# The loads of a phase re-ordered, and two deferred mean projections pinned behind the first output matmuls

## The chip, the cores and the metric

The kernel runs on one core of one Trainium2 chip, as one program in one launch. The metric is the device time of the execution in microseconds (us). A kernel is timed in several executions, and the kernel before is always timed on the same chip in the same rounds.

## The reference

The kernel computes two independent parts from two inputs and puts their results side by side, `[1, 2048, 2048]` in bf16.

```python
# part A: a diagonal state-space layer (S5), x is [1, 2048, 1024]
h = Lam_bar * h + Bu[t]                              # for each of the 2048 steps t
y = 2.0 * einsum('blp,dp->bld', hseq, Cmat).real + x * Dskip

# part B: attention in 64 segments of 32 tokens, 32 heads of 128, with 8 memory tokens in front
h = concatenate([mem, xs])                           # 40 rows
q, k, v = h @ Wq, h @ Wk, h @ Wv
o = softmax(mask(q @ k.T * scale)) @ v @ Wo
mem = o[:8]                                          # memory of the next segment
# ... result: concatenate([y, o[8:] of all segments], axis=-1)
```

Part B's recurrence over the memory is avoided in this kernel: it guesses the memory of every segment from the mean of the segment's values, and checks the guess at the end. Those means are what this text calls a *mean group*: for 4 heads, 32 matmuls of 128x64 that multiply `Wv` by the mean token of each segment. The result (`b_ogT`) is multiplied by `Wo` in eight *Wo groups* to give the guess.

## The kernel before

Time runs through four phases. Phase 1 computes the states of part A (kept in device memory, `a_hs`) and most values of part B. **Phase 2**, about 361 to 495 us, is the one that the change touches: the output matmuls of part A, with the guess of part B woven in. Then come projections with attention, and the output projection.

Part A in phase 2 is a generator. It yields after each *half*: 16 matmuls of 128x512 into one PSUM buffer of the tag "O", and the eviction from PSUM into the output tile `a_ot`. Two halves make an output tile of 128 rows, which is then stored.

```python
    def ps(self, tag, shape=(128, 512), dt=FP32):
        return self.psp.tile(list(shape), dt, name="ps" + tag, bufs={"P": 3, "S": 2, "R": 1, "O": 2}[tag])
# ... (cut)
    def stage2(self, pool):
        k = self.k; V, G, PE = k.V, k.G, k.PE
        q0 = k.G
        # ... (cut: Dskip, and load_xn, which loads 128 rows of x into a_xn2, 3 buffers)
        for tb in range(NB):                        # 4 blocks of 512 rows
            hl = []
            for q in range(4):                      # states of the block: 4 tiles of 0.5 MB, 2 buffers
                hl.append(pool.tile([128, 2, 2, TB], BF16, name=f"a_hl{q}", bufs=2))
                (q0 if tb == 0 else k.SP).dma_start(hl[q][:], self.hs[tb][:, 2 * q:2 * q + 2, :, :])
            for tt in range(4):                     # 4 output tiles of 128 rows
                t0 = tb * TB + tt * 128
                xn = xns.pop(4 * tb + tt)
                xd = pool.tile([128, D], FP32, name="a_xd", bufs=2)
                G.tensor_tensor(xd[:], xn[:], dB[:], ALU.mult)
                ot = pool.tile([128, D], BF16, name="a_ot", bufs=2)
                for half in range(2):
                    hs = slice(half * 512, (half + 1) * 512)
                    py = k.ps("O")
                    # ... (cut: 16 matmuls of the states with CT into py)
                    V.tensor_tensor(ot[:, hs], py[:], xd[:, hs], ALU.add)
                    yield
                k.SP.dma_start(self.out[0, t0:t0 + 128, 0:D], ot[:])
                if 4 * tb + tt + 3 < TT:
                    load_xn(4 * tb + tt + 3, k.SP)
```

Note for later: `a_ot` has two buffers, the store of a finished tile is issued from SyncE (`k.SP`), and nearly all loads of the phase are issued from SyncE as well.

The body of the phase weaves the two deferred mean groups (`og`), the Wo groups (`guess`, which loads its four 2 MB pieces `b_wog` itself) and the first `Wq`/`Wk` load in between:

```python
            g = b.guess(p2)
            s2 = a.stage2(p2)
            wv = [wv, b.load_wv(1)]
            for i, _ in enumerate(s2):
                if i in (2, 4):
                    b.og(i // 2 - 1, wv[i // 2 - 1], "P")
                if i > 4 and i % 2 == 1:
                    next(g, None)
                if i == 16:
                    b.load_wqk(0)
            for _ in g:
                pass
            b.v_mem(0, wv[0])
            b.v_mem(1, wv[1])
```

The order of the source is not the order on the engines: a scheduler orders each engine's instructions, unless one is pinned with `keep_in_program_order`. In the kernel before it puts both deferred mean groups ahead of all halves.

Of the kernel before, what the change touches and what calls it, by code (L numbers as in the profile page):

```python
# [9 lines left out]
BF16 = mybir.dt.bfloat16  # L10
# [15 lines left out]
H = 32; E = 128; SEG = 32; M = 8; NSEG = 64; L = M + SEG  # L26
# [95 lines left out]
class PartA:  # L122
# [137 lines left out]
# [4 lines that stand above are left out]
        dB = pool.tile([128, D], BF16, name="a_dB", bufs=1)  # L264
        q0.dma_start(dB[:], self.Dskip.unsqueeze(0).to_broadcast([128, D]))
        xns = {}

        def load_xn(t, q):
            xns[t] = pool.tile([128, D], BF16, name="a_xn2", bufs=3)
            q.dma_start(xns[t][:], self.x[0][t * 128:(t + 1) * 128, :])  # L270
        for t in range(3):
            load_xn(t, q0)
        for tb in range(NB):
            hl = []
            for q in range(4):
                hl.append(pool.tile([128, 2, 2, TB], BF16, name=f"a_hl{q}", bufs=2))
                (q0 if tb == 0 else k.SP).dma_start(hl[q][:], self.hs[tb][:, 2 * q:2 * q + 2, :, :])
            for tt in range(4):
                t0 = tb * TB + tt * 128
                xn = xns.pop(4 * tb + tt)  # L280
# [6 lines that stand above are left out]
                    for pc in range(PC):  # L287
                        for i in range(2):
                            PE.matmul(py[:], hl[pc // 2][:, pc % 2, i, tt * 128:(tt + 1) * 128], self.CT[:, i, pc, hs],  # L289
                                      start=(pc == 0 and i == 0), stop=(pc == PC - 1 and i == 1))  # L290
                    V.tensor_tensor(ot[:, hs], py[:], xd[:, hs], ALU.add)  # L291
                    yield
                k.SP.dma_start(self.out[0, t0:t0 + 128, 0:D], ot[:])
                if 4 * tb + tt + 3 < TT:
                    load_xn(4 * tb + tt + 3, k.SP)



class PartB:
# [96 lines left out]
    def og(self, hb, w, tag="R"):  # L396
        k = self.k
        p = k.ps(tag)
        for h in range(4):
            for c in range(KC):  # L400
                k.PE.matmul(p[:, h * NSEG:(h + 1) * NSEG], w[:, c, h * 128:(h + 1) * 128], self.xbar[:, c, :], start=(c == 0), stop=(c == KC - 1))
        k.V.tensor_copy(self.ogT[:, hb * 4:(hb + 1) * 4, :], p[:, 0:4 * NSEG].rearrange("p (h s) -> p h s", h=4))


    def guess(self, pool):
        k = self.k; V, PE = k.V, k.PE
        pg = k.ps("S")
        for q in range(4):
            wo = pool.tile([128, H, 256], BF16, name="b_wog", bufs=2)
            k.SP.dma_start(wo[:], self.Wo[:, :, q * 256:(q + 1) * 256])  # L410
            for dc in range(2):
                c = 2 * q + dc
                for h in range(H):
                    PE.matmul(pg[:, c * NSEG:(c + 1) * NSEG], wo[:, h, dc * 128:(dc + 1) * 128], self.ogT[:, h, :], start=(h == 0), stop=(h == H - 1))
                yield
        pv = pg[:].rearrange("p (c s) -> p c s", c=KC)
        m = self.memT
        V.tensor_copy(m[:, :, NMX + 1:NMX + 2], pv[:, :, 0:1])
        V.tensor_copy(m[:, :, NMX + 3:NM], pv[:, :, 1:NSEG])

        gx = pool.tile([128, KC, NM], BF16, name="b_gx", bufs=1)
        V.tensor_copy(gx[:, :, 0:2], pv[:, :, 0:2])
        V.tensor_copy(gx[:, :, 2:NTL - 1], pv[:, :, 1:NSEG])
        V.tensor_copy(gx[:, :, NTL - 1:NM], pv[:, :, 0:1].to_broadcast([128, KC, NMX + 1]))
        pt = k.ps("R", (128, 1024), BF16)
        for c in range(KC):
            PE.transpose(pt[0:NM, c * 128:(c + 1) * 128], gx[:, c, :], k.ident[:])
        V.tensor_copy(self.gm[:], pt[0:NM, :])
        yield
# [325 lines left out]
def kernel_main(tc, A_x, A_Lre, A_Lim, A_Bre, A_Bim, A_Cre, A_Cim, A_logdt, A_Dskip, B_x, B_mem0, B_Wq, B_Wk, B_Wv, B_Wo, out,  # L755
                force=False, dbg=None):
    with ExitStack() as ctx:
        k = K(tc, ctx)
# [4 lines left out]
        b = PartB(k, B_x, B_mem0, B_Wq, B_Wk, B_Wv, B_Wo, out)  # L763

        def pool(name, side, bufs=2):
            return tc.tile_pool(name=name, bufs=bufs, side=side, reuse_waits="tile")
# [8 lines left out]
        with pool("p1", "right") as p1:  # L775
            a.tab = a.tmp = a.wp = a.btp = p1
            wv = b.load_wv(0)
# [9 lines left out]
            for pc in range(PC):  # L787
                v = b.v_x(pc, wv)
                nxt = None
                for tb in range(NB):  # L790
# [7 lines left out]
                    if tb == 1:  # L798
                        nxt = b.load_wv((pc + 1) % PC)
# [23 lines left out]
                wv = nxt  # L823
# [7 lines left out]
        with pool("p2", "right") as p2:  # L831
            g = b.guess(p2)
            s2 = a.stage2(p2)
            wv = [wv, b.load_wv(1)]
            for i, _ in enumerate(s2):
                if i in (2, 4):
                    b.og(i // 2 - 1, wv[i // 2 - 1], "P")
                if i > 4 and i % 2 == 1:
                    next(g, None)
                if i == 16:  # L840
                    b.load_wqk(0)
            for _ in g:
                pass
            b.v_mem(0, wv[0])
            b.v_mem(1, wv[1])
# [49 lines left out]
@with_exitstack  # L895
def kernel(
    ctx: ExitStack,
    tc: tile.TileContext,
    A_x: bass.AP,
    A_Lambda_re: bass.AP,  # L900
    A_Lambda_im: bass.AP,
    A_B_re: bass.AP,
    A_B_im: bass.AP,
    A_C_re: bass.AP,
    A_C_im: bass.AP,
    A_log_dt: bass.AP,
    A_Dskip: bass.AP,
    B_x: bass.AP,
    B_mem0: bass.AP,
    B_Wq: bass.AP,  # L910
    B_Wk: bass.AP,
    B_Wv: bass.AP,
    B_Wo: bass.AP,
    B_seg_len: bass.AP,
    out: bass.AP,
):
    assert int(B_seg_len) == SEG
    kernel_main(tc, A_x, A_Lambda_re, A_Lambda_im, A_B_re, A_B_im, A_C_re, A_C_im, A_log_dt, A_Dskip,
                B_x, B_mem0, B_Wq, B_Wk, B_Wv, B_Wo, out)
# [35 lines left out]
```

## Time and profile before

| kernel before | |
|---|---|
| time | 1315.48 us median of 3 runs (1314.9 to 1315.63) |
| profiled span, mean granted clock | 1312.2 us, 0.992 |
| TensorE busy, whole | 1267.0 us (97%) |
| phase 2, start of its first mean group to start of the memory values | 360.26 to 494.59, 134.33 us |
| TensorE idle in phase 2 | 11.4 us (134.33 less 122.95 busy) |

The busy table of the page (time, share of the span, instructions) says that TensorE is the engine to look at:

```profile
PE 1267.0 (97%) x7808; PEld 658.2 (50%) x7874; DVE 673.7 (51%) x1500; ACT 427.1 (33%) x1135; POOL 211.4 (16%) x291
```

The list of waits of TensorE in phase 2 (what waited, for what, total us, times, longest) has one large entry:

```profile
PE psP L401 <- DMA b_wv<-in_B_Wv_dram: 10.0, 1, 10.0
PE psP L401 <- ACT b_vst L62: 0.5, 1, 0.5
```

The timeline of TensorE shows where it lies (start, us, line, operation; in brackets the idle time before it and what ended it):

```profile
360.26 1.10 PE L401 MATMUL psR<-b_xbar,b_wv 128*128 128x64 bf16 x32
361.90 1.09 PE L401 MATMUL psP<-b_xbar,b_wv 128*128 128x64 bf16 x32 [0.54 <-ACT b_vst L62]
372.99 1.89 PE L401 MATMUL psP<-b_xbar,b_wv 128*128 128x64 bf16 x32 [9.99 <-DMA b_wv<-in_B_Wv_dram]
374.69 0.61 PE L289 MATMUL psO<-t_105,a_hl_3617 128*128 128x512 bf16 x1
...
494.59 3.62 PE L437 MATMUL psP<-b_wv,b_xe 128*73 128x512 bf16 x16
```

The third mean group stands 10 us for its `Wv`, and the output matmuls (`psO`), which need nothing of it, queue up behind it. The last line, the memory values (128x73), ends the phase.

The timeline of SyncE's queue shows the issues (start, how long the issue took, line, transfer). The `Wv` load goes out only at 367.07.

```profile
367.07 0.54 SPq L370 DMA_DIRECT2D b_wv<-in_B_Wv_dram  x1
367.93 0.38 SPq L410 DMA_DIRECT2D b_wog<-in_B_Wo_dram  x1
368.36 8.01 SPq L277 DMA_DIRECT2D a_hl_3928<-a_hs_71  x1
...
378.32 0.42 SPq L277 DMA_DIRECT2D a_hl_3934<-a_hs_71  x1
384.00 0.34 SPq L293 DMA_DIRECT2D out_dram<-a_ot  x1
```

Two evictions of VectorE in the phase:

```profile
383.28 0.69 DVE L291 TENSOR_TENSOR a_ot<-psO,a_xd 128x512 bf16<-128x512 f32 x1 [0.96 <-PE psO L289]
...
393.69 0.69 DVE L291 TENSOR_TENSOR a_ot<-psO,a_xd 128x512 bf16<-128x512 f32 x1 [2.82 <-PE psO L289]
```

The table of stretches of 6 us (length; busy us and instructions of PE, PEld, DVE, ACT, POOL; granted TensorE clock; share of the DMA engines; GB/s) shows the second cost of the gap, a clock of about half speed:

```profile
366.00:372.00 6.00, 0.00 (x0) 0.00 (x0) 0.10 (x1) 0.00 (x0) 0.00 (x0) 0.62 0.79 239
372.00:378.00 6.00, 4.79 (x40) 2.97 (x42) 0.42 (x1) 0.00 (x0) 0.00 (x0) 0.53 1.16 294
...
384.00:390.00 6.00, 5.95 (x29) 2.69 (x29) 0.69 (x1) 0.00 (x0) 2.13 (x1) 1.00 0.87 284
```

The Trainium skill ("TensorE: Matmul & The Clock Gate", Part 1) says that about 3.4 us of idling halves the clock and about 3.4 us of work restores it. The trace agrees in kind: TensorE idles from 363.0, the granted clock is 0.50 from about 368, and it is back at about 377.7, some 4.7 us after work resumed.

### The profile page before, as it was taken

The page shows a single profiled execution, that of the slowest core. Times are in us where ns is not written, and L with a number is a line of the kernel's source. Part 1 is how long each engine was busy: PE and PEld are TensorE (multiplying, and loading weights), DVE is VectorE, ACT ScalarE, POOL GpSimd, SP SyncE. Part 2 cuts the span into 40 slices and gives each one's busy share as a digit, 9 for nine tenths or more (in the row PEclk, how much of TensorE's full clock was granted, in tenths as well). Part 3 has the DMA queues.
Part 4 walks back from the last instruction along what each step waited for, and adds up shares of the span by engine and source line. Part 5 has one row for each costly group of instructions (what it writes and reads, how often), then busy time and mean ns, then how long its engine had stood idle before and what let it go on. Part 6 is the DMA issues. An engine that isn't in the chain of part 4 may idle for free. (4 is left out here: it accounts for less than half of the span.)

```text
span 1312.2 us, 20083 instructions
## 1 busy us (share of the span) xinstructions
PE 1267.0 (97%) x7808; PEld 658.2 (50%) x7874; DVE 673.7 (51%) x1500; ACT 427.1 (33%) x1135; POOL 211.4 (16%) x291
## 2 busy tenths in 40 slices
PE   6899899999969999999999999999999989999997
PEld 2344444444435545555555555555555544444443
DVE  6999998988821224555555555545555530001000
ACT  3333333343210001554544454544544540001000
POOL 5000000000112221222222222222222220000000
PEclk9999999999989999999999999999999989999999
DMA  9993443344389519323343434333333470403000
GB/s 227 262 215 105 121 127 101 110 129 144 121 263 311 172 48 262 85 84 110 99 133 99 133 99 133 99 87 98 86 90 78 142 240 18 136 18 127 16 21 21
DMA packets 230939, 163.15 MB, mean 124 GB/s; under 512 B 74976, under 2 KB 214864, under 8 KB 230840
## 3 DMA queue, kind: packets, MB, share of 16 engines
q1 hardware_dynamic: 229368, 158.18, 42.2%
q0 software_dynamic: 1408, 3.61, 0.9%
q8 instruction: 63, 1.03, 0.3%
q14 instruction: 36, 0.29, 0.1%
q10 hardware_dynamic: 64, 0.02, 0.0%
HBM read 95.72 MB, written 49.30 MB: 111 GB/s over the span
## 5 line engine op out<-in xcount | busy, mean ns | idle before, releaser
L383 PE MATMUL psP<-b_wv,b_xe 128*128 128x512 bf16 x1024 | 229.8, 381 | 16.0 <-DMA b_xe<-in_B_x_dram 11.2
L519 ACT ACTIVATE b_e<-psS 99x396 bf16<-99x396 f32 x176 | 88.2, 501 | 416.8 <-PE psS L516 413.6
L522 POOL TENSOR_TENSOR b_m<-b_e,maskB 99x396 bf16<-99x396 bf16 x160 | 139.4, 871 | 352.9 <-ACT b_e L519 352.9
L542 DVE TENSOR_TENSOR b_ot<-psO,b_r 128x384 bf16<-128x384 f32 x176 | 98.1, 558 | 189.2 <-ACT b_r L536 170.4
L383 PEld LDWEIGHTS <-b_xe 128*128 128x128 bf16 x1024 | 100.0, 98 | 139.3 <-DMA b_xe<-in_B_x_dram 12.7
L607 PEld LDWEIGHTS <-b_ol 128*128 128x128 bf16 x896 | 87.8, 98 | 106.3 <-issue 1.7
L64 DVE CAST b_ost<-psP 128x512 bf16<-128x512 f32 x16 | 11.1, 692 | 193.4 <-PE psP L607 193.4
L62 ACT ACTIVATE b_vst<-psP 128x512 bf16<-128x512 f32 x128 | 73.8, 586 | 97.0 <-PE psP L383 82.8
L607 PE MATMUL psP<-t_4704,b_ol 128*128 128x512 bf16 x438 | 99.6, 381 | 0.7 <-issue 0.2
L607 PE MATMUL psP<-wo_12095,b_ol 128*128 128x512 bf16 x438 | 98.8, 379 | 0.5
L536 ACT ACTIVATE b_r<-b_ln 128x396 f32<-128x396 f32 x176 | 94.0, 534 | 5.4
L535 ACT ACTIVATE b_ln<-psR 128x396 f32<-128x396 f32 x176 | 86.9, 494 | 0.0
L62 ACT ACTIVATE b_ost<-psP 128x512 bf16<-128x512 f32 x16 | 9.6, 597 | 211.2 <-PE psP L607 198.0
L291 DVE TENSOR_TENSOR a_ot<-psO,a_xd 128x512 bf16<-128x512 f32 x32 | 22.1, 692 | 95.6 <-PE psO L289 88.2
L64 DVE CAST b_k_4709<-psP 128x480 bf16<-128x480 f32 (+2 forms) x96 | 48.8, 529 | 31.1 <-PE psP L492 30.6
L540 PE MATMUL psO<-b_m,b_v 99*128 99x99 bf16 x704 | 61.4, 209 | 0.8 <-DMA b_v<-b_vx_74 0.8
L531 PE MATMUL psR<-b_m,ones 99*128 99x396 bf16 x176 | 59.2, 336 | 3.1 <-POOL b_m L522 2.2
L64 DVE CAST b_k_4717<-psP 128x480 bf16<-128x480 f32 (+2 forms) x96 | 48.7, 528 | 21.2 <-PE psP L492 21.2
L540 PEld LDWEIGHTS <-b_v 99*128 99x128 bf16 x704 | 50.6, 98 | 14.3 <-DMA b_v<-b_vx_74 1.1
L64 DVE CAST b_q_4705<-psP 128x480 bf16<-128x480 f32 (+2 forms) x96 | 48.7, 528 | 17.2 <-PE psP L492 17.2
L64 DVE CAST b_q_4713<-psP 128x480 bf16<-128x480 f32 (+2 forms) x96 | 48.6, 528 | 12.5 <-PE psP L492 12.5
L248 ACT ACTIVATE a_gr<-a_wr 128x512 bf16<-128x512 f32 x32 | 20.2, 630 | 72.1 <-DVE a_wr L237 72.1
(724 smaller groups left out, 1950.2 us busy)
## 6 DMA issues: line engine op xcount, KB each, us to landing
b_wv<-in_B_Wv_dram SPq DMA_DIRECT2D x16, 1024.0 KB
b_wog<-in_B_Wo_dram SPq DMA_DIRECT2D x4, 2048.0 KB
out_dram<-a_ot SPq DMA_DIRECT2D x16, 256.0 KB
t_4704<-in_B_Wo_dram SPq DMA_DIRECT2D x1, 4096.0 KB
b_ol<-b_os_90 SPq DMA_DIRECT2D x4, 1024.0 KB
b_ol<-b_os_91 SPq DMA_DIRECT2D x4, 1024.0 KB
b_ol<-b_os_92 SPq DMA_DIRECT2D x4, 1024.0 KB
wo_12095<-in_B_Wo_dram SPq DMA_DIRECT2D x1, 4096.0 KB
```

The lines of the kernel that those rows point to most:

```text
L62: self.S.activation(out, in_, ACT.Copy)
L64: self.V.tensor_copy(out, in_)
L291: V.tensor_tensor(ot[:, hs], py[:], xd[:, hs], ALU.add)
L383: k.PE.matmul(p[:], self.xe[:, c, t * 128:(t + 1) * 128], w[:, c, :], start=(c == 0), stop=(c == KC - 1))
L519: k.S.activation(e[:], s[0:GW], ACT.Exp, scale=float(E) ** -0.5, accum_out=self.accE[0:GW, i:i + 1])
L522: k.G.tensor_tensor(m[:], e[:], mask[0:GW, :, :].unsqueeze(2).to_broadcast([GW, 2, 2, GW]), ALU.mult)
L531: PE.matmul(sm[:, 0:W4], k.ones[0:GW, :], mf, start=True, stop=True)
L535: k.S.activation(ln[:], sm[:, 0:W4], ACT.Ln)
L536: k.S.activation(r[:].rearrange("p a b q -> p (a b q)"), ln[:], ACT.Exp, scale=-1.0, accum_out=self.accR[:, i:i + 1])
L540: PE.matmul(o[:, gg, hh, :], vt[:, 2 * u + gg, hh * 128:(hh + 1) * 128], m[:, gg, hh, :], start=True, stop=True)
L542: V.tensor_tensor(ot[:, :, 2 * u * GX:(2 * u + 2) * GX].rearrange("p h (g n) -> p g h n", n=GX), o[:, :, :, 0:GX], r[:, :, :, 0:GX], ALU.mult)
L607: PE.matmul(p[:], lhs, self.wo[half][:, h, :], start=(h == 0), stop=(h == H - 1))
```

## The change

The intent is to issue the loads of phase 2 in the order in which they are needed. The states of a block are loaded during the block in front of it, the four `Wo` pieces are spaced out, and the two deferred mean groups are pinned behind halves 4 and 6, so that TensorE has work while their `Wv` is on its way. Their evictions move from VectorE to ScalarE. Nothing is computed more or less than before.

```diff
@@ stage2
-        for tb in range(NB):
+
+        def load_h(tb, q0):
             hl = []
             for q in range(4):
                 hl.append(pool.tile([128, 2, 2, TB], BF16, name=f"a_hl{q}", bufs=2))
-                (q0 if tb == 0 else k.SP).dma_start(hl[q][:], self.hs[tb][:, 2 * q:2 * q + 2, :, :])
+                k.tc.keep_in_program_order(q0.dma_start(hl[q][:], self.hs[tb][:, 2 * q:2 * q + 2, :, :]))
+            return hl
+        nxt = load_h(0, q0)
+        for tb in range(NB):
+            hl = nxt
             for tt in range(4):
@@ end of a tile, after its store and the load of an x tile
+                if tt == 0 and tb + 1 < NB:
+                    nxt = load_h(tb + 1, k.SP)
@@ og
-                k.PE.matmul(p[...], w[...], self.xbar[:, c, :], ...)
-        k.V.tensor_copy(self.ogT[:, hb * 4:(hb + 1) * 4, :], ...)
+                mm = k.PE.matmul(p[...], w[...], self.xbar[:, c, :], ...)
+                if tag == "P" and h == 0 and c == 0:
+                    k.tc.keep_in_program_order(mm)
+        k.copy("s" if tag == "P" else "v", self.ogT[:, hb * 4:(hb + 1) * 4, :], ...)
@@ new: load_wog (the Wo piece's load taken out of guess, and pinned)
+            self.k.tc.keep_in_program_order(self.k.SP.dma_start(wo[:], self.Wo[:, :, q * 256:(q + 1) * 256]))
@@ the body of the phase
             for i, _ in enumerate(s2):
-                if i in (2, 4):
-                    b.og(i // 2 - 1, wv[i // 2 - 1], "P")
-                if i > 4 and i % 2 == 1:
-                    next(g, None)
-                if i == 16:
+                if i in (3, 5):
+                    b.og((i - 3) // 2, wv[(i - 3) // 2], "P")
+                if i in (5, 8, 12, 15):
+                    b.load_wog((5, 8, 12, 15).index(i), p2)
+                if i in (10, 12, 14, 16, 18, 20, 22, 24):
+                    next(g)
+                if i == 20:
                     b.load_wqk(0)
```

More of the change, by code (lines that the diff above doesn't have):

```diff
@@ L400, in og, with load_wog @@
             for c in range(KC):
-                k.PE.matmul(p[:, h * NSEG:(h + 1) * NSEG], w[:, c, h * 128:(h + 1) * 128], self.xbar[:, c, :], start=(c == 0), stop=(c == KC - 1))
-        k.V.tensor_copy(self.ogT[:, hb * 4:(hb + 1) * 4, :], p[:, 0:4 * NSEG].rearrange("p (h s) -> p h s", h=4))
+                mm = k.PE.matmul(p[:, h * NSEG:(h + 1) * NSEG], w[:, c, h * 128:(h + 1) * 128], self.xbar[:, c, :], start=(c == 0), stop=(c == KC - 1))
+                if tag == "P" and h == 0 and c == 0:
+                    k.tc.keep_in_program_order(mm)
+        k.copy("s" if tag == "P" else "v", self.ogT[:, hb * 4:(hb + 1) * 4, :], p[:, 0:4 * NSEG].rearrange("p (h s) -> p h s", h=4))
+    def load_wog(self, q, pool):
+        wo = pool.tile([128, H, 256], BF16, name="b_wog", bufs=2)
+        self.k.tc.keep_in_program_order(self.k.SP.dma_start(wo[:], self.Wo[:, :, q * 256:(q + 1) * 256]))
+        self.wog.append(wo)
     def guess(self, pool):
@@ L408, in guess @@
         for q in range(4):
-            wo = pool.tile([128, H, 256], BF16, name="b_wog", bufs=2)
-            k.SP.dma_start(wo[:], self.Wo[:, :, q * 256:(q + 1) * 256])
+            wo = self.wog.pop(0)
             for dc in range(2):
@@ L834, in kernel_main @@
             wv = [wv, b.load_wv(1)]
+            b.wog = []
             for i, _ in enumerate(s2):
-                if i in (2, 4):
-                    b.og(i // 2 - 1, wv[i // 2 - 1], "P")
-                if i > 4 and i % 2 == 1:
-                    next(g, None)
-                if i == 16:
+                if i in (3, 5):
[5 more added lines that the diff above has]
+                if i == 20:
                     b.load_wqk(0)
```

## The prediction

> **What bounds the kernel now.** The page's busy table gives TensorE 1267.0 of 1312.2 us (97%); VectorE has 51%, ScalarE 33%. The change touches only the second phase (output matmuls of part A, about 361 to 495 us). There the stretch table and the timeline show TensorE without a gap, except one: the waits list has the mean projection `psP L401 <- DMA b_wv`, 10.0 us, once. In order of time: the first mean group (psR) ends at 361.4; TensorE waits 0.54 us for ScalarE to free a PSUM buffer, runs the second group, then stands from 363.0 to 372.99 for the second `b_wv` load, which SyncE issues only at 367.07. The output matmuls behind it don't need that load: the state tiles of block 0 were issued by 354.9 and take 4.6 to 6.1 us. The granted clock falls to 0.50 at about 368 and returns at about 377.7, so the third mean group takes 1.65 us instead of 0.93 (loss 0.7), and the block's first 13 matmuls 4.29 us instead of 2.81 (loss 1.5). The Trainium skill ("TensorE: Matmul & The Clock Gate", Part 1: about 3.4 us idle halves the clock, about 3.4 us of work restores it) states the same; this trace agrees.
>
> **What the change does.** By the order of instructions, TensorE goes straight from the first mean group to the block's matmuls; the two deferred mean groups stand after 4 and 6 halves. No matmul is added or removed. Two 128x256 evictions move from VectorE to ScalarE, idle 148 us there. On the queue, the four Wq/Wk loads (2 MB) now come right behind `b_wv`, ahead of block 1's states: not the "order of need", since the unpinned prefetch was hoisted. The first Wo piece comes behind the states.
>
> **Cost.** A half takes 3.454 us (eight take 27.63 at the phase's end). Estimate of the new phase: 32 x 3.454 + 8 Wo groups x 0.93 + 2 mean groups x 0.95 + transposes 0.45 = 120.3 us. Before: 494.6 - 361.4 = 133.2. Saving 12.9 us: 10.0 idle, 2.2 half clock, 0.5 PSUM wait, rounding. TensorE is the chain, and later phases keep their order, so nearly all reaches the end.
>
> **Do loads come in time?** The queue moved about 290 GB/s with the Wo piece outstanding and about 400 with the states. Estimate: `b_wv` lands at 373 (needed 383), Wq/Wk by 380, block 1's states 386 (needed 391), first Wo piece 395 (needed 401), second 403 (needed 417), block 2's states 409 (needed 421). The tightest slack is 5 us: no new TensorE wait over 1 us. Spacing Wo gives nothing by itself: before, no Wo piece or state tile was waited for.
>
> **Prediction.** 1315.5 - 12.9 = 1302.6 us (1% less); range 1299.5 to 1305.5. Chances: faster by over 2% 0.01, within 2% 0.98, slower 0.01.
>
> **What the profile would show.** Right: no TensorE wait for `b_wv`; first output matmul at about 361.5; granted clock 1.00 throughout 360 to 380; the memory-value matmuls (128x73) start at about 481.7; TensorE busy down by about 2 us, idle down by about 10.5. Wrong: a wait for block 1's states near 391, for a Wo piece near 401, or for an output buffer because `a_xd` on POOL lacks its x tile.
>
> **What would make it wrong.** Wq/Wk transfers slower than the Wo piece was, so that block 1 waits and, past 3.4 us, the clock falls again; or the attention phase, 13 us earlier, waiting longer for its values than 0.8 us now at 519.5.

## The result, and the profile after

| | before | after |
|---|---|---|
| time, median | 1315.56 us of 4 runs (1314.9 to 1317.98) | 1309.34 us of 4 runs (1308.32 to 1312.89) |
| ratio of fast runs, 95% interval | | 0.9954 [0.9932, 0.9977] |
| phase 2 | 134.33 us | 129.57 us |
| TensorE busy and idle in phase 2 | 122.95 and 11.4 us | 123.30 and 6.3 us |

A ratio is the mean time of one kernel's fast runs over that of the other's of the same rounds, so it is not quite the ratio of the medians that stand beside it. Executions over 1.5% slower than the fastest of the same kernel are left out of the means.

The change is worth half a per cent, about 6 us, where 12.9 us (1302.6 us) had been predicted. The median lies above the predicted range, 1299.5 to 1305.5 us. More than half of what was to be gained is missing. The busy table shows TensorE no less busy; two evictions have gone from VectorE to ScalarE, as intended:

```profile
PE 1267.7 (97%) x7806; PEld 657.6 (50%) x7874; DVE 672.5 (51%) x1498; ACT 428.3 (33%) x1137; POOL 211.8 (16%) x291
```

The waits of TensorE and of VectorE in phase 2 show that the wait for `b_wv` is gone, and that another is there, for an output tile `a_ot`, which itself waits for a store:

```profile
PE psO L294 <- DVE a_ot L296: 5.3, 2, 4.9
DVE a_ot L296 <- DMA out_dram<-a_ot: 28.9, 4, 12.2
```

The timeline of TensorE:

```profile
360.05 1.10 PE L408 MATMUL psR<-b_xbar,b_wv 128*128 128x64 bf16 x32
360.98 13.98 PE L294 MATMUL psO<-t,a_hl 128*128 128x512 bf16 x62
374.79 1.10 PE L408 MATMUL psP<-b_xbar,b_wv 128*128 128x64 bf16 x32
375.73 7.07 PE L294 MATMUL psO<-t,a_hl 128*128 128x512 bf16 x31
382.63 1.10 PE L408 MATMUL psP<-b_xbar,b_wv 128*128 128x64 bf16 x32
388.59 0.59 PE L294 MATMUL psO<-t,a_hl 128*128 128x512 bf16 x1 [4.86 <-DVE a_ot L296]
...
405.74 3.61 PE L294 MATMUL psO<-t,a_hl 128*128 128x512 bf16 x16 [0.45 <-DVE a_ot L296]
...
489.62 3.62 PE L450 MATMUL psP<-b_wv,b_xe 128*73 128x512 bf16 x16
```

Up to 383 this is what was predicted, to about 0.5 us: output matmuls from 360.98, mean groups after 4 and 6 halves, no gap. Then, where half 6 should start, TensorE stands for 4.86 us. The timeline of VectorE (the evictions) names the buffer. Tile 0 is complete at 368.09 + 0.69 = 368.78. Tile 2 takes the same buffer, and its first eviction goes only at 387.85, after 12.16 us in which VectorE waited for a store:

```profile
368.09 0.69 DVE L296 TENSOR_TENSOR a_ot<-psO,a_xd 128x512 bf16<-128x512 f32 x1 [1.92 <-PE psO L294]
...
374.99 0.69 DVE L296 TENSOR_TENSOR a_ot<-psO,a_xd 128x512 bf16<-128x512 f32 x1 [2.69 <-PE psO L294]
387.85 1.29 DVE L296 TENSOR_TENSOR a_ot<-psO,a_xd 128x512 bf16<-128x512 f32 x2 [12.16 <-DMA out_dram<-a_ot]
```

The timeline of SyncE's queue shows why the store was late:

```profile
366.87 0.54 SPq L377 DMA_DIRECT2D b_wv<-in_B_Wv_dram  x1
367.46 0.61 SPq L475 DMA_DIRECT2D b_wq<-in_B_Wq_dram  x1
...
375.82 1.89 SPq L278 DMA_DIRECT2D a_hl<-a_hs  x4
377.81 0.38 SPq L298 DMA_DIRECT2D out_dram<-a_ot  x1
...
379.74 0.38 SPq L415 DMA_DIRECT2D b_wog<-in_B_Wo_dram  x1
380.41 11.08 SPq L298 DMA_DIRECT2D out_dram<-a_ot  x1
391.59 0.89 SPq L270 DMA_DIRECT2D a_xn<-in_A_x_dram  x2
```

Tile 0 could be stored from 368.8 on, but SyncE issues in its own order, and in front of the store stood the four `Wq`/`Wk` loads, an x tile and the states: the store went out at 377.81. (The compiled program holds it back a second time: the store shares a completion semaphore, a counter by which a transfer reports its end, with the first `Wk` load, and waits for that load, which landed at 376.09.) Behind these it took another 10.0 us (377.81 to 387.85) until VectorE had the buffer back. The landings, which the packed trace records and no view shown here prints, tell why: the last of the four state tiles in front landed at 385.45, the store at 387.73. So 19 us lie between "tile 0 complete" and "its buffer free", while TensorE fills two more output tiles in 4 halves of 3.454 us. Two `a_ot` buffers and two PSUM buffers cover that only up to 383.6.

The stretches show the stall and what it did to the clock:

```profile
378.00:384.00 6.00, 5.73 (x55) 3.06 (x53) 0.00 (x0) 0.23 (x1) 2.13 (x1) 1.00 1.06 384
384.00:390.00 6.00, 1.19 (x3) 0.54 (x4) 1.29 (x2) 0.15 (x1) 0.73 (x1) 0.78 1.11 336
390.00:396.00 6.00, 6.00 (x20) 2.23 (x18) 0.00 (x0) 0.00 (x0) 1.39 (x1) 0.66 1.09 316
```

In 390 to 396, TensorE is "6.00 busy", but the row counts 20 matmuls, where a stretch of output matmuls at full clock counts 29 or 30 (29 in 384 to 390 before the change). The half clock of the kernel before was not removed; it was moved 20 us to the right.

The phase as one stretch, before and then after, gives the account:

```profile
360.26:494.59 134.33, 122.95 (x860) 62.08 (x872) 29.36 (x49) 4.00 (x6) 29.75 (x14) 0.96 0.64 194
```

```profile
360.05:489.62 129.57, 123.30 (x858) 61.46 (x872) 27.97 (x47) 4.77 (x8) 29.69 (x14) 0.97 0.66 201
```

The phase is 4.76 us shorter: idle time fell by 5.1 us (11.4 to 6.3), and busy time rose by 0.35. (Some matmul records are missing here: 858 to 860 of 873. The traces of e1 to e4 below have all 873, and e1 shows 121.38 us busy where e5, with 859, shows 120.43. So about 0.9 us of the "idle" time here is work; it cancels where two such traces are compared.) The prediction had idle down by 10.5 and busy down by about 2.

### The profile page after: what moved, and what is told of

Its sections match the earlier page's. It is cut to its first block, busy times and chain, and to the rows that moved or that the text cites. A ratio compares the mean times of both kernels' runs of the same rounds, so it can differ in the third digit from the quotient of the medians.

```text
span 1307.5 us, 20082 instructions
## 1 busy us (share of the span) xinstructions
PE 1267.7 (97%) x7806; PEld 657.6 (50%) x7874; DVE 672.5 (51%) x1498; ACT 428.3 (33%) x1137; POOL 211.8 (16%) x291
## 5 line engine op out<-in xcount | busy, mean ns | idle before, releaser
L505 PE MATMUL psP<-b_xe,b_wq 128*128 128x480 bf16 x1024 | 222.9, 366 | 0.0
L505 PE MATMUL psP<-b_xe,b_wk 128*128 128x480 bf16 x1024 | 222.9, 366 | 0.0
L505 PEld LDWEIGHTS <-b_wk 128*128 128x128 bf16 x1024 | 97.1, 98 | 95.8
L505 PEld LDWEIGHTS <-b_wq 128*128 128x128 bf16 x1024 | 95.7, 98 | 87.9
L64 DVE CAST b_k<-psP 128x480 bf16<-128x480 f32 (+1 forms) x192 | 97.5, 529 | 52.0 <-PE psP L505 51.4
L294 PE MATMUL psO<-t,a_hl 128*128 128x512 bf16 x497 | 114.2, 385 | 6.3 <-DVE a_ot L296 5.3
L64 DVE CAST b_q<-psP 128x480 bf16<-128x480 f32 (+1 forms) x192 | 97.3, 528 | 29.6 <-PE psP L505 29.6
L620 PE MATMUL psP<-t,b_ol 128*128 128x512 bf16 x438 | 100.4, 383 | 0.7 <-issue 0.2
L620 PE MATMUL psP<-wo,b_ol 128*128 128x512 bf16 x438 | 98.8, 379 | 0.5
L294 PEld LDWEIGHTS <-a_hl 128*128 128x128 bf16 x512 | 50.0, 99 | 65.5 <-issue 9.3
```

The source lines that it names most:

```text
L64: self.V.tensor_copy(out, in_)
L294: PE.matmul(py[:], hl[pc // 2][:, pc % 2, i, tt * 128:(tt + 1) * 128], self.CT[:, i, pc, hs], start=(pc == 0 and i == 0), stop=(pc == PC - ...
L505: PE.matmul(p[:, 0:480], w[i][:, c, hh * 128:(hh + 1) * 128], self.xe[:, c, 480 * q:480 * q + 480], start=(c == 0), stop=(c == KC - 1))
L620: PE.matmul(p[:], lhs, self.wo[half][:, h, :], start=(h == 0), stop=(h == H - 1))
```

## The experiments

**Theory.** The new stall is the output store's. Outputs now begin 13.7 us earlier (360.98 against 374.69), into a queue that still holds the loads of the whole neighbourhood. The store of tile 0 sits behind them, and two `a_ot` buffers don't span the delay.

**Rivals.** (1) The unpinned `Wq`/`Wk` loads, hoisted by the scheduler to 367.46, are the whole cause, and without them there is no stall. (2) The x tiles come late (issued at 391.59), so `a_xd` on POOL is missing; this is what the prediction had named as the danger. (3) The re-ordered loads cost something by themselves, and the pinned means alone would give the full gain.

e1 to e4 ran on one chip, e5 to e8 on a second chip, each time with the kernel before beside them: 1317.03 us median of 11 runs (1313.67 to 1318.67) on the first, 1315.94 us of 11 runs (1313.53 to 1317.96) on the second. All eight gave correct results.

| kernel | median us (runs) | ratio to before, 95% | phase 2, us | TensorE's wait for `a_ot`, us |
|---|---|---|---|---|
| before | | | 134.33 | none |
| the change | 1309.34 (4) | 0.9954 [0.9932, 0.9977] | 129.57 | 5.3 |
| e7, the change again | 1310.30 (5) | 0.9962 [0.9949, 0.9975] | 129.57 | 5.3 |
| e1, third `a_ot` buffer | 1304.62 (4) | 0.9904 [0.9889, 0.9919] | 121.67 | 0.3 |
| e2, `Wq`/`Wk` late | 1305.24 (5) | 0.9912 [0.9899, 0.9926] | 122.33 | 0.9 |
| e3, stores from ScalarE | 1303.87 (4) | 0.9906 [0.9892, 0.9921] | 121.42 | none |
| e4, before + pinned means only | 1313.34 (6) | 0.9970 [0.9957, 0.9983] | 129.74 | 5.6 |
| e6, load order only | 1315.01 (6) | 1.0002 [0.9985, 1.0019] | 133.87 | none (9.9 for `b_wv`) |
| e8, e4 + third `a_ot` buffer | 1303.67 (5) | 0.9913 [0.9900, 0.9927] | 121.21 | none |
| e5, e1 and e2 together | 1301.48 (4) | 0.9892 [0.9878, 0.9907] | 121.22 | none |

### e1: a third output buffer

On the changed kernel. (Four buffers do not fit: the build says that the pool would need 89.2 KB per partition where 87.8 are left.)

```diff
-                ot = pool.tile([128, D], BF16, name="a_ot", bufs=2)
+                ot = pool.tile([128, D], BF16, name="a_ot", bufs=3)
```

> The changed kernel with three a_ot buffers instead of two (four do not fit in SBUF). Theory T (an output tile cannot be evicted because the store of the tile two before it is still queued behind 4 MB of loads; a_ot has two buffers, the PSUM output has two, so TensorE stops, and then runs at half clock): TensorE's wait for a_ot (4.9 + 0.4 us) falls below 1 us, granted clock 1.00 from 384 to 396, memory-value matmuls start near 482 instead of 489.6, time about 1302.5 (1301 to 1304.5). Rival X (the late x tiles on POOL are the cause: a_xd waited 9.5 us for a_xn): an extra a_ot buffer changes nothing, about 1309.

Measured: 1304.62 us, phase 121.67 us, 7.9 us shorter than the change's. The waits of TensorE and of POOL in the phase:

```profile
PE psO L294 <- DVE a_ot L296: 0.3, 1, 0.3
```

```profile
POOL a_xd L287 <- DMA a_xn<-in_A_x_dram: 15.2, 2, 9.7
```

One buffer more, with all loads and stores where they were, takes the stall away. POOL still waited for the late x tiles, 15.2 us in all, and TensorE did not notice: rival 2 falls.

### e2: the `Wq`/`Wk` loads late

On the changed kernel, the loads for the first two head pairs are pinned at halves 20 and 22. (The source of the change has the first at half 20 and the second at the start of the projections.)

```diff
-    def load_wqk(self, hp):
+    def load_wqk(self, hp, pin=False):
@@
-                self.k.SP.dma_start(w[:], self.Wf[i][:, :, hp * 256:(hp + 1) * 256])
+                d = self.k.SP.dma_start(w[:], self.Wf[i][:, :, hp * 256:(hp + 1) * 256])
+                if pin:
+                    self.k.tc.keep_in_program_order(d)
@@ proj
-            self.load_wqk(hp + 1)
+            if hp > 0:
+                self.load_wqk(hp + 1)
@@ the body of the phase
                 if i == 20:
-                    b.load_wqk(0)
+                    b.load_wqk(0, True)
+                if i == 22:
+                    b.load_wqk(1, True)
```

> The changed kernel with the four Wq/Wk loads (2 MB) pinned at halves 20 and 22 instead of hoisted ahead of block 1's states. Theory T: any 2 MB less in front of the first store brings it about 7 us earlier, to about 380 us; tile 2 then is evicted before TensorE needs the buffer at 383.6, its wait falls below 1 us, time about 1302.5 to 1304. Rival W (the hoisted Wq/Wk loads as such are the cause) expects the same here; it differs from T in the run with the deferred means alone. Rival X: x tiles come earlier too, so the same. Rival B (the block 1 states are what is in front) would leave the wait: the store still follows them.

Measured: 1305.24 us, phase 122.33 us. With 2 MB less in front of it, tile 0's store went out at 370.42 and landed at 379.32, and the eviction of tile 2 that follows waited only for TensorE:

```profile
370.42 0.38 SPq L298 DMA_DIRECT2D out_dram<-a_ot  x1
```

```profile
379.55 0.69 DVE L296 TENSOR_TENSOR a_ot<-psO,a_xd 128x512 bf16<-128x512 f32 x1 [3.75 <-PE psO L294]
```

What is left on TensorE is another tile's wait: tile 4 needs the buffer of tile 2, whose store stood behind the second `Wo` piece and landed at 397.73.

```profile
PE psO L294 <- DVE a_ot L296: 0.9, 1, 0.9
```

So without the hoisted loads in front of the first store, the stall of 4.86 us does not occur in the changed kernel. Whether they are *the* cause, or merely what happened to stand in front, e4 decides. The stall of 0.9 us left the granted clock at 1.00 (stretch 396 to 402), where that of 4.86 us halved it, again in agreement with the Trainium skill ("TensorE: Matmul & The Clock Gate", Part 1).

### e3: the stores from another queue

On the changed kernel, the 16 stores of the phase are issued from ScalarE, and nothing else moves.

```diff
-                k.SP.dma_start(self.out[0, t0:t0 + 128, 0:D], ot[:])
+                k.S.dma_start(self.out[0, t0:t0 + 128, 0:D], ot[:])
```

> The changed kernel with the 16 output stores of part A issued from ScalarE instead of SyncE, loads unchanged. Theory T (order within one queue): the stores no longer stand behind the loads, land some 3 to 5 us after their tile is evicted, no wait for a_ot, time about 1302.5 (1301 to 1304.5). Rival D (the DMA engines are simply full, about 300 to 400 GB/s, and any transfer is late): stores still land some 15 us late, the wait of about 5 us stays, about 1309.

Measured: 1303.87 us, phase 121.42 us, 8.2 us shorter, with no wait of TensorE at all. But not in the way that was expected. The timelines of ScalarE's queue and of VectorE:

```profile
376.73 4.62 ACTq L298 DMA_DIRECT2D out_dram<-a_ot  x2
```

```profile
383.60 1.29 DVE L296 TENSOR_TENSOR a_ot<-psO,a_xd 128x512 bf16<-128x512 f32 x2 [7.34 <-DMA out_dram<-a_ot]
```

The buffer came free about 14 us after tile 0's second eviction ended, not 3 to 5. The store was issued at 376.73, hardly sooner than from SyncE: the compiled program puts a wait in front of it, on the completion semaphore that it shares with the first `Wk` load, and that load landed at 376.66, just before. The changed kernel has this wait too, so another engine alone could not issue the store much sooner. What did shorten was the time from issue to the freed buffer: 6.9 us (376.73 to 383.60) in place of 10.0. That was just in time, since TensorE would have stood from about 384.1.

Two statements of the Trainium skill meet here. "DMA: Bandwidth & Descriptors", Queues, rings and completion order, gives SyncE and ScalarE each a queue row of their own, with rings on the same 16 DMA engines, between which an engine takes turns. The 6.9 against 10.0 us agree with that. The section "Issuing engines are not separate DMA queues" of the same page says that issuing from several engines "will only save the time on the sequencer it takes to initiate the DMA". Here it saved 8.2 us of TensorE's time. Two advantages came together: 3.1 us after the issue, and, counted from the start of the first mean group, an issue 1.7 us earlier (16.1 against 17.8 us). The recorded landings show the part after the issue: from SyncE the store landed behind all four state tiles (the last at 385.45, the store at 387.73); from ScalarE it landed at 383.48, ahead of three of the four (384.06, 385.48 and 388.64). What either part would be worth alone, no run tests.

### e4: the pinned means alone

On the kernel before: the pinned, deferred mean groups with their evictions on ScalarE, and no change to any load.

```diff
-                k.PE.matmul(p[...], w[...], self.xbar[:, c, :], ...)
-        k.V.tensor_copy(self.ogT[...], ...)
+                mm = k.PE.matmul(p[...], w[...], self.xbar[:, c, :], ...)
+                if tag == "P" and h == 0 and c == 0:
+                    k.tc.keep_in_program_order(mm)
+        k.copy("s" if tag == "P" else "v", self.ogT[...], ...)
@@ the body of the phase
-                if i in (2, 4):
-                    b.og(i // 2 - 1, wv[i // 2 - 1], "P")
-                if i > 4 and i % 2 == 1:
+                if i in (3, 5):
+                    b.og((i - 3) // 2, wv[(i - 3) // 2], "P")
+                if i > 5 and i % 2 == 1:
```

> The kernel before with only the two mean groups deferred (pinned after halves 4 and 6, evicted on ScalarE); loads as before: b_wv, first Wo piece (2 MB), block 1's states, then the first store. Theory T: the gap for b_wv goes, but the store stands behind the Wo piece and the states and lands near 387, so a wait for a_ot of about 4 to 6 us and the half clock appear here too: about 1308 to 1310, as the whole change. Rival W (only the hoisted Wq/Wk loads did the harm): no wait, about 1302.5.

Measured: 1313.34 us, phase 129.74 us: the same phase as with the whole change, and the same stall. The waits of TensorE and VectorE, and the stretch of the half clock:

```profile
PE psO L289 <- DVE a_ot L291: 5.6, 1, 5.6
```

```profile
DVE a_ot L291 <- DMA out_dram<-a_ot: 24.1, 3, 12.9
```

```profile
390.00:396.00 6.00, 3.14 (x8) 1.17 (x8) 1.29 (x2) 0.00 (x0) 2.12 (x1) 0.64 1.16 299
```

In this kernel no `Wq`/`Wk` load stands in front of store 0; the 2 MB `Wo` piece and the states do, as in the kernel before. Store 0 went out 18.4 us after the start of the first mean group (382.06 less 363.62), where it was 17.8 in the changed kernel (377.81 less 360.05). Rival 1 falls: the hoist is one way to fill the queue, and the loads of the kernel before are another that is just as good. The stall belongs to the early start of the outputs. Rival 3 falls with it: the means alone do not give the full gain.

### e6: the order of the loads alone

On the changed kernel, the mean groups go back to where they were: not pinned, at halves 2 and 4, evicted on VectorE.

```diff
-                mm = k.PE.matmul(...)
-                if tag == "P" and h == 0 and c == 0:
-                    k.tc.keep_in_program_order(mm)
-        k.copy("s" if tag == "P" else "v", self.ogT[...], ...)
+                mm = k.PE.matmul(...)
+        k.copy("v", self.ogT[...], ...)
@@ the body of the phase
-                if i in (3, 5):
-                    b.og((i - 3) // 2, wv[(i - 3) // 2], "P")
+                if i in (2, 4):
+                    b.og(i // 2 - 1, wv[i // 2 - 1], "P")
```

> The change's new order of loads alone; mean groups unpinned after halves 2 and 4, evicted on VectorE, as before. Theory T: TensorE's 10 us wait for b_wv and the half clock stay as before; the first store is ready about 13 us later, so no wait for a_ot: phase about 134 us, time equal to the kernel before within 1.5 us. Rival L (the new order of loads is worth something by itself): 2 us or more faster than before.

Measured: 1315.01 us, ratio 1.0002 [0.9985, 1.0019], phase 133.87 us. The old wait is back, in full:

```profile
PE psP L408 <- DMA b_wv<-in_B_Wv_dram: 9.9, 1, 9.9
```

So the re-ordering of the loads, which gives the change its name, is worth nothing by itself, within 0.2%. Without the pinned means there is no gain; with them alone (e4) there is about the gain of the whole change.

### e7: the change once more

No edit; the changed kernel beside the others on the second chip.

> The changed kernel once more, beside the others on one chip: ratio to before 0.995 to 0.996 again, TensorE wait for a_ot near 5 us. If the deferred means alone (0.9970) are really slower than the whole change, this shows about 2 us less than that run; if the two are the same, it shows about 0.997.

Measured: 1310.30 us, ratio 0.9962 [0.9949, 0.9975], phase 129.57 us to the hundredth, the same wait of 5.3 us. The interval of e4, [0.9957, 0.9983], overlaps with this one: whether the load order adds a little on top of the means is not settled by the times, and the phases (129.57 and 129.74 us) put it at 0.2 us.

### e8 and e5: the stall removed, without and with the load changes

e8 is e4 with a third buffer, so the kernel before with two edits and no load changed:

```diff
 (e4, and)
-                ot = pool.tile([128, D], BF16, name="a_ot", bufs=2)
+                ot = pool.tile([128, D], BF16, name="a_ot", bufs=3)
```

> The kernel before with the deferred means and three a_ot buffers, no change to any load. Theory T: the third buffer absorbs the late store here too, TensorE's wait for a_ot under 1 us, phase about 121.5 to 122.5 us, time about 0.990 to 0.992 of before: the load part of the change is not needed for the gain. Rival L (the spacing of the loads matters by itself): a wait for states or a Wo piece of more than 2 us remains.

e5 is the changed kernel with the edits of e1 and e2 together:

```diff
 (e2, and)
-                ot = pool.tile([128, D], BF16, name="a_ot", bufs=2)
+                ot = pool.tile([128, D], BF16, name="a_ot", bufs=3)
```

> Both cures at once: Wq/Wk pinned at halves 20 and 22, and three a_ot buffers. Theory T: no TensorE wait over 0.3 us in the second phase; from the first mean group's start to the memory-value matmuls 121.4 us (the sum of the work), against 121.7 and 122.3 with one cure each, so about 1302 to 1304 and not measurably better than either. If something else still held the phase, the two cures would add up and give several us more.

Measured: e8 1303.67 us, e5 1301.48 us (1301.46 to 1302.64). The whole phase as one stretch, of e8 and then of e5:

```profile
361.18:482.39 121.21, 120.43 (x858) 60.86 (x872) 28.49 (x47) 4.77 (x8) 29.66 (x14) 1.00 0.70 215
```

```profile
361.80:483.02 121.22, 120.43 (x859) 60.82 (x872) 28.14 (x47) 4.77 (x8) 29.73 (x14) 1.00 0.70 215
```

The two phases are the same to 0.01 us, TensorE is busy in all but 0.8 us of them (and these are about what the missing matmul records would fill), and the clock is 1.00 throughout. The 2 us between the medians of e5 and e8 are not explained by the phase, and the intervals of their ratios overlap ([0.9878, 0.9907] and [0.9900, 0.9927]); they stay open. e5 has the lowest time of all kernels here and beats both the kernel before (by 14 us of medians) and the changed one (by 8 us or more). What it has over e8 in the trace is slack: in e5 VectorE never waited for a store, in e8 it did for 15.6 us in all.

These runs also settle the account of the changed kernel. Against e5, its phase is 129.57 - 121.22 = 8.35 us too long: 5.5 us of idle time (6.27 less 0.79: the waits of 4.86 and 0.45, and 0.22 behind them) and 2.9 us of busy time at half clock (123.30 less 120.43).

## Why the prediction was wrong, point by point

- **What bounds the kernel, and the sum of what could be won: right.** It gave 12.9 us for the phase, from 10.0 us idle, 2.2 us half clock and 0.5 us PSUM wait. With the stall out of the way, e5 and e8 have a phase 13.1 us shorter, and busy time in it down by 2.5 us. e5's median of 1301.48 us is within 1.1 us of the predicted 1302.6.
- **TensorE goes on to the output matmuls after the first mean group: right.** They start at 360.98 (predicted 361.5), there is no wait for `b_wv`, and the clock is 1.00 from 360 to 380.
- **The loads come in time: right as far as it went.** TensorE waited for no state tile and no `Wo` piece, and the attention, 13 us earlier in the best kernels, did not wait longer for its values (0.8 us before, 0.6 in e5).
- **"The tightest slack is 5 us: no new TensorE wait over 1 us": this is the step that failed.** The paragraph followed each load through the queue to the matmul that needs it. The 16 stores of the output go through the same queue, and they were not in the sum. Its landing times for the loads just in front and behind were good to 1 us: 386 was estimated for block 1's states, which landed at 385.45, and 395 for the first `Wo` piece, which landed at 395.36. Tile 0's store was issued between these two, so the same sum, had it listed the store, would have put it at about 387 (our estimate: 386 and 256 KB at 400 GB/s); it landed at 387.73. A store has a deadline too: it must hand its buffer back before the second tile after it is evicted. For tile 0, complete at 368.8, that was about 379, when half 4 was done, with some 5 us more from the two PSUM buffers; the buffer came at 387.85. The cost was 5.5 us of idle time and 2.9 us of half clock, which is the whole of the difference of 8.35 us.
- **The warning was on the right buffer for the wrong reason.** The prediction said that a wait for an output buffer would show if `a_xd` lacked its x tile. An output buffer was waited for, but it lacked the store of the tile before; e1 shows `a_xd` late by more than this, without a stall.
- **Why the kernel before had no such wait, though it had the same two buffers and as full a queue:** its gap of 10 us had hidden the matter. Its first tile was complete at 384.0, when the last states had been issued 5.3 us before (378.74), and the DMA share of 384 to 390 was down to 0.87. Its store was issued at once and landed at 387.27. The eviction that needed the buffer, the first of tile 2 at 393.69, waited only for TensorE. To remove the gap was to move the first store into the fullest part of the queue. This is shown by e4, which changes the means and no load, and stalls.
- **"Spacing Wo gives nothing by itself": right,** and more widely than said, since the whole re-ordering of loads gives nothing measurable by itself (e6). It even put as much in front of the first store as it took away: with the hoisted `Wq`/`Wk` in place of the `Wo` piece, the stall is 4.86 us in place of 5.6.
- **"TensorE busy down by about 2 us": wrong in the whole, for two reasons.** In the phase, it rose by 0.35 since the half clock only moved. In the totals it could not have been seen anyway: the unchanged stretch in front of the phase has 338.9 us of TensorE busy time in the trace of the change, and 343.2 in that of e5. The memory values start at 489.62, where 481.7 was predicted.
- **The range was too narrow** for what it was based on. It allowed for run-to-run spread on a sum whose terms were all gains; a new wait of one buffer's length was counted only as a remote case.

## What to carry to other kernels

When idle time in front of a producer of output is removed, its stores start earlier, into whatever the queue holds at that moment: list the stores of the stretch with the loads, and give each a deadline, the time at which its buffer is needed again. If outputs share a queue with bulk loads, the output buffers must cover the time from a finished tile to its free buffer, or the stores need another way out. Here that time was 19.1 us (368.78 to 387.85). Two `a_ot` and two PSUM buffers covered 14.8 us (368.8 to 383.6), and a third `a_ot` buffer adds a tile of two halves, 6.9 us: 21.7 us by this estimate, and e1 bears it out. One buffer more, or another issuing engine, each won back about 8 us here. An expected gain that comes in at less than half is worth a look at the waits list right behind the place that was repaired: the same 10 us had become 5.5 us of another wait and the same half clock 20 us later.

## What the Trainium skill lacked or had wrong

- "DMA: Bandwidth & Descriptors", Issuing engines are not separate DMA queues: the statement that issuing from several engines "will only save the time on the sequencer" is too narrow here. Moving 16 stores from SyncE to ScalarE shortened the phase from 129.57 to 121.42 us, and not by the time of issue alone: the first store took 6.9 us from issue to freed buffer in place of 10.0. The suggestion of "Perfetto Trace Analysis", DMA Optimizations, that it may make sense to give inputs and outputs separate issuing engines agrees with this run; the two pages pull in different directions.
- "DMA: Bandwidth & Descriptors": we found nothing there on how long an issue of a core's own load or store holds its engine while much is outstanding on the queue. SyncE was held for 11.08 us in the issue of one store behind a 2 MB `Wo` load (and for 8.01 us in the kernel before, in the issue of one state tile behind such a load). That the queue was full is our reading; no run tests it alone. What follows in SyncE's order, the x tiles here, is issued only after it (at 391.59).
- No page we read says how many output buffers a store in a shared queue needs. Here two gave 5.3 us of waits on TensorE and three gave 0.3 (e1); in the changed kernel 19 us lay between the completion of the first tile and its free buffer.
